# One staging ring of seven SBUF buffers, and the conversions' shifted word in PSUM throughout, in a fused attention, FFN and mixture-of-experts kernel

## The chip, the cores and the metric

The program runs on one core of one Trainium2 chip. The metric is the device time of one execution in microseconds (us). The kernel before takes 1338.55 us (median of 3 runs, 1336.74 to 1340.67). The engines are called PE (TensorE), DVE (VectorE), ACT (ScalarE), POOL (GpSimd) and SP (SyncE, which issues the DMAs here).

## What is computed

```python
scores = q @ k.T / sqrt(64)                       # 4 batches, 8 heads, 576 x 576
kth    = np.partition(scores, -32)[..., -32]      # the 32nd largest of each row
attn   = softmax(where(scores >= kth, scores, -1e9))
x      = (attn @ v) as 2304 rows of 512
x      = relu(x @ w_in) ** 2 @ w_out              # d_ff 2048, w_in and w_out in float64
# the two best of 8 experts of each row by noisy logits, and then
out   += weight * (relu(x @ w1[e]) @ w2[e])       # d_ff 1024
```

## The kernel before

**Attention.** The work is cut into 80 units; a unit is a pair of heads for one tile of 128 queries (or for the 64 left-over queries of a batch). Each head of a full unit, and each left-over unit as a whole, is one *search*, 144 in all: PE makes the scores (L439), ACT evacuates them (L442), DVE finds the 32nd largest (`max` L453, `match_replace` L457 and what follows, ending in a `reduce_max`, L494), POOL and ACT make the masked exponentials (POOL L506, ACT L510, POOL L511, ACT L512), PE transposes them (L523), ACT copies them out (L525), and PE multiplies by the values (L564).

**Staging of keys and queries.** Keys and queries are loaded in float32 into staging tiles, `kn` for two heads of keys (L408 and L409, two buffers) and `qn` for four heads of queries (L423 and L424, two buffers), and then split into a rounded high part (ACT, L400) and a remainder (DVE or POOL, L401). One `qn` serves the four searches of a tile's half of the heads; it is called a query group below.

**Conversions.** The FFN's weights come as float64. `convert` (from L144) makes float32 of one 128 by 512 block: a load of 512 KB into `raw` (four buffers), ACT scales the high words into a tile `high` (L153), DVE shifts `high` in place (L155) and joins the sign to it (L156), ACT scales the low words (L157), POOL adds them (L158), and SP stores the block to DRAM (`whole`, L159). There are 32 such conversions. For the first 14 (`IN_PSUM`), `high` is a bank of the pool `ps_acc` in PSUM (three banks in rotation); for the last 18 it is the SBUF tile `ca` itself.

**FFN.** It runs in seven chunks of 2, 2, 2, 3, 3, 3 and 3 tiles of 128 rows as background work between the steps of attention. Chunk 0 reads `whole` in float32 (L351, L315); chunk 1 reads `whole` into the same four `raw` buffers, splits it and stores the two parts (L336 to L342); later chunks read those. The accumulators of a chunk are banks of `ps_acc`, one for each tile, and so are the banks that `route` uses behind each chunk for its transposes and logits. Then come the experts (from 667 us).

**What sets the order.** Each engine runs its instructions in a fixed order, which is found when the program is built: the Python code gives instructions and priorities, a scheduler orders them by a timeline of its own, and buffers of a pool are given out in turn. All loads and stores of the lines above stand in one queue, SP's.

Of the kernel before, what the change touches and what calls it, by code (L numbers as in the profile page):

```python
# [8 lines left out]
F32 = mybir.dt.float32  # L9
# [18 lines left out]
CONVERTS = 3  # L28
IN_PSUM = 14
LEFT_WEIGHT = 0.6  # L30
# [24 lines left out]
def attention_ffn_moe(ctx: ExitStack, tc: tile.TileContext, q, k, v, w_ffn, w_route, noise, w_exp, out,  # L55
# [66 lines left out]
    ps_acc = wctx.enter_context(tc.tile_pool(name="ps_acc", bufs=3, space=PSUM))  # L122

    def late_consts():
        nc.sync.dma_start(wg, w_route)
        nc.sync.dma_start(nz, noise)
# [15 lines left out]


    def convert(vpool, f, which):  # L144
        n = DM
        raw = vpool.tile([P, 2 * n], U32, name="raw", bufs=4 if keep is not None else 2)
        nc.sync.dma_start(raw, w_ffn[f, which])
        pair = raw.rearrange("p (j t) -> p j t", t=2)
        lo_w, hi_w = pair[:, :, 0], pair[:, :, 1]
        a = vpool.tile([P, n], U32, name="ca", bufs=4 if keep is not None else 2)  # L150

        high = ps_acc.tile([P, DM], F32, name="acc") if 2 * f + which < IN_PSUM else a.bitcast(F32)
        nc.scalar.activation(high, hi_w.bitcast(F32), AF.Copy, scale=2.0 ** -112)  # L153
        high = high.bitcast(U32)
        nc.vector.tensor_scalar(high, high, 3, None, op0=ALU.logical_shift_left)  # L155
        nc.vector.scalar_tensor_tensor(a, hi_w, 0x80000000, high, op0=ALU.bitwise_and, op1=ALU.bitwise_or)  # L156
        nc.scalar.activation(lo_w, lo_w, AF.Copy, scale=2.0 ** -29)  # L157
        nc.gpsimd.tensor_tensor(a, a, lo_w, op=ALU.add)  # L158
        nc.sync.dma_start(whole[f][:, which], a.bitcast(F32))  # L159
# [27 lines left out]
    def route(t0, xrs):  # L187
# [3 lines left out]
        if after:  # L191
            bank = lambda: after[0].tile([P, DM], F32, name="acc2")
            xts = [mpools[0].tile([P, NC, P], F32, name="xts", bufs=CT) for _ in xrs]
        else:
            bank = lambda: ps_acc.tile([P, DM], F32, name="acc")
            xts = [fpool.tile([P, NC, P], F32, name="xt", bufs=2) for _ in xrs]
# [104 lines left out]
    def ffn(t0, nt, xT):  # L301
# [4 lines left out]
        def second(f, wo, gt):  # L306
            if f == 0:
                while fronts:
                    front()
                acc.extend(ps_acc.tile([P, DM], F32, name="acc") for _ in range(nt))  # L310
            for tt in range(nt):
# [14 lines left out]
        for f in range(NF):  # L326
# [7 lines left out]
            elif divide:  # L334
                raw = vpools[0].tile([P, 2 * DM], U32, name="raw", bufs=4 if keep is not None else 2).bitcast(F32)
                nc.sync.dma_start(raw, whole[f].rearrange("p a d -> p (a d)"))  # L336
# [66 lines left out]
    def prep_k(b, g, j):  # L403
# [3 lines left out]
        for h in ([2 * j], [2 * j + 1]) if (b, g) == (0, 0) else ([2 * j, 2 * j + 1],):  # L407
            kn = apool.tile([P, 2, S], F32, name="kn", bufs=2)[:, 0:len(h), :]  # L408
            nc.sync.dma_start(kn, k[b, 4 * g + h[0]:4 * g + h[-1] + 1].rearrange("h p s -> p h s"))  # L409
            dst = K4[b, g][:, h[0]:h[-1] + 1, :]  # L410
            for i in range(len(h)):
                split(nc.vector if (b, g) == (0, 0) else nc.gpsimd, dst[:, i], dst[:, i], kn[:, i], D)

# [7 lines left out]
    def prep_q(b, g, s0):  # L421

        qn = apool.tile([P, 4, P], F32, name="qn", bufs=2)  # L423
        nc.sync.dma_start(qn.rearrange("p h s -> p (h s)"), q[b, s0 // P, g])  # L424
# [227 lines left out]
    def expert(e, parts, ahead):  # L652
# [14 lines left out]
        for n, t in enumerate(tiles_):  # L667
            acc[t] = ps_acc.tile([P, DM], F32, name="acc") if n < 3 else ps_m.tile([P, DM], F32, name="acc2")

# [315 lines left out]
    def beyond(e, row):  # L985
# [23 lines left out]
        nc.scalar.copy(xt, pt.rearrange("p (c s) -> p c s", c=NC))  # L1009
        acc = ps_acc.tile([P, DM], F32, name="acc")  # L1010
        for f in range(NFE):
# [116 lines left out]
```

## Time and profile before

| | us |
|---|---|
| median of 3 runs | 1338.55 |
| the profiled execution, its own time | 1336.86 |
| its span in the trace | 1335.1 |
| PE busy | 1241.5 (93%) |
| DVE busy | 899.2 (67%) |
| ACT busy | 856.6 (64%) |
| POOL busy | 746.2 (56%) |
| mean granted PE clock | 0.985 of full speed |

The busy shares are averages over stages with different limits: in attention all engines are in use, in the experts' part mostly PE. The span lacks 1.8 us of the profiled execution's own time, which lie around it.

### The profile page before, as it was taken

How to read it: one execution, taken by the hardware profiler on the slowest of the kernel's cores; microseconds unless marked ns; L12 is line 12 of the kernel's file. 1: busy time of each engine (PE TensorE's matmuls, PEld its weight loads, DVE VectorE, ACT ScalarE, POOL GpSimd, SP SyncE). 2: the span in 40 equal slices, each digit the busy share in tenths (PEclk: the TensorE clock that was granted, in tenths of full speed). 3: DMA queues.
4: the chain of work that ended last, by engine and by line, in shares of the span. 5: the costliest groups of instructions: out<-in, count | busy, mean ns of one | idle time of the engine just before them, and what ended most of it. 6: DMA issues, size and time to landing. Idle time of an engine off the chain costs nothing.

```text
span 1335.1 us, 26136 instructions
## 1 busy us (share of the span) xinstructions
PE 1241.5 (93%) x8030; PEld 1071.8 (80%) x8030; DVE 899.2 (67%) x4557; ACT 856.6 (64%) x1886; POOL 746.2 (56%) x1243
## 2 busy tenths in 40 slices
PE   3769889989998999999999999999999999999997
PEld 2556667777887888888888888899899999988886
DVE  8999989998986899978677410255534343444554
ACT  6878879989897889987878653543433333332443
POOL 5857798887786676767655635333432241503221
PEclk9889999999999999999999999999999999999999
DMA  9998886875675554366534689366643443534464
GB/s 333 361 368 292 274 273 235 309 260 181 219 231 193 166 174 157 106 211 204 168 115 158 205 297 332 113 198 197 192 151 117 143 136 119 174 103 143 141 202 140
DMA packets 93302, 270.06 MB, mean 202 GB/s; under 512 B 11612, under 2 KB 11740, under 8 KB 93152
## 3 DMA queue, kind: packets, MB, share of 16 engines
q1 hardware_dynamic: 83872, 239.91, 54.3%
q0 software_dynamic: 9280, 28.40, 5.9%
q8 instruction: 65, 1.06, 0.3%
q14 instruction: 85, 0.70, 0.2%
HBM read 209.90 MB, written 60.45 MB: 202 GB/s over the span
## 4 chain that ended last, share of the span: by engine, by line
PE 61%; ACT 13%; DVE 11%; DMA 7%; issue 5%; POOL 3%; SPq 0%; POOLq 0%; DVEq 0%; ACTq 0%
PE pa L564 5%; PE ph L693 5%; PE ph L695 4%; PE ph L694 4%; PE acc L676 4%; PE acc L674 4%; PE acc L675 4%; PE ps L439 4%; PE pa L523 3%; PE acc L322 3%; PE acc L320 3%; PE acc L321 3%; DMA raww<-in_exp 3%; PE pf L357 2%; PE pf L358 2%
## 5 line engine op out<-in xcount | busy, mean ns | idle before, releaser
L511 POOL TENSOR_TENSOR sb<-sb,w 128x576 f32<-128x576 f32 x144 | 205.8, 1430 | 63.3 <-ACT w L510 59.3
L453 DVE MAX8 m<-sb 128x8 f32<-128x115 f32 (+1 forms) x720 | 190.3, 264 | 53.1 <-ACT sb L442 47.6
L457 DVE MATCH_REPLACE8 w<-m,sb 128x115 f32<-128x115 f32 (+1 forms) x720 | 187.1, 263 | 0.0
L699 ACT ACTIVATE ht<-ph 128x384 fp32r<-128x384 f32 (+1 forms) x128 | 55.8, 436 | 195.2 <-PE ph L695 177.0
L715 POOL DMA_INDIRECT out<-y,info x40 | 45.1, 1127 | 242.4 <-DVE y L714 224.7
L439 PE MATMUL ps<-K,qt 128*128 128x288 f32 (+2 forms) x640 | 131.4, 333 | 43.9 <-ACT sb L442 30.0
L700 DVE SCALAR_TENSOR_TENSOR ht<-ph,ht 128x384 fp32r<-128x384 f32 (+1 forms) x128 | 62.7, 490 | 161.7 <-ACT ht L699 148.5
L693 PE MATMUL ph<-xe,wi 128*128 128x256 f32 (+1 forms) x512 | 159.9, 312 | 1.9 <-ACT wi L686 1.0
L695 PE MATMUL ph<-xe,wi 128*128 128x256 f32 (+1 forms) x512 | 159.2, 311 | 0.2 <-DVE wi L687 0.2
L694 PE MATMUL ph<-xe,wi 128*128 128x256 f32 (+1 forms) x512 | 158.9, 310 | 0.0
L439 PEld LDWEIGHTS ps<-K,qt 128*128 128x128 f32 x640 | 103.7, 204 | 64.4 <-ACT sb L442 37.7
L512 ACT ACTIVATE sb<-sb,keep 128x576 f32<-128x576 f32 x144 | 112.5, 781 | 28.1 <-POOL sb L511 27.6
L674 PE MATMUL acc<-wo,ht 128*128 128x512 f32 x320 | 125.8, 397 | 0.4 <-DVE y L714 0.4
L675 PE MATMUL acc<-wo,ht 128*128 128x512 f32 x320 | 125.3, 395 | 0.0
L510 ACT ACTIVATE w<-sb,keep 128x576 f32<-128x576 f32 x144 | 111.3, 775 | 16.4 <-POOL keep L506 16.2
L371 POOL TENSOR_TENSOR gt<-r,gt 128x384 fp32r<-128x384 f32 (+1 forms) x96 | 90.7, 946 | 53.2 <-ACT gt L370 39.9
L481 DVE MAX8 m<-w 128x8 f32<-128x288 f32 x288 | 116.0, 443 | 0.1
L357 PE MATMUL pf<-xT,wi 128*128 128x384 f32 (+1 forms) x320 | 106.0, 331 | 5.4 <-ACT r L364 3.9
L523 PE MATMUL pa<-ident,sb 128*128 128x128 f32 x576 | 94.8, 289 | 16.5 <-ACT sb L512 7.1
L676 PE MATMUL acc<-wo,ht 128*128 128x512 f32 x320 | 108.9, 401 | 0.0
L525 ACT COPY pt<-pa 128x512 f32<-128x512 f32 x144 | 83.2, 578 | 32.1 <-PE pa L523 21.2
L693 PEld LDWEIGHTS ph<-xe,wi 128*128 128x128 f32 x512 | 96.4, 188 | 8.5 <-ACT wi L686 1.4
(211 smaller groups left out, 3511.9 us busy)
## 6 DMA issues: line engine op xcount, KB each, us to landing
raww<-in_exp SPq DMA_DIRECT2D x88, 512.0 KB
wi<-wsc SPq DMA_DIRECT2D x64, 512.0 KB
wo<-wsc SPq DMA_DIRECT2D x64, 512.0 KB
raw<-in_ffn SPq DMA_DIRECT2D x32, 512.0 KB
xs<-xr SPq DMA_DIRECT2D x40, 258.0 KB
mr<-xs SPq DMA_DIRECT2D x40, 258.0 KB
qn<-in_q SPq DMA_DIRECT2D x40, 256.0 KB
whole<-ca SPq DMA_DIRECT2D x32, 256.0 KB
```

What stands on the lines that cost most here:

```text
L357: nc.tensor.matmul(ph[:, 0:n], wi[:, 0, sl], xT[:, 0, c, 0:n], start=(c == 0), stop=False)
L439: nc.tensor.matmul(ps[:, n, 0:w], st, kt[:, at:at + w], start=(i == 0), stop=(i == len(pairs) - 1))
L453: in_turn(nc.vector.max(parts[i][1], sb[:, parts[i][0]]))
L457: in_turn(nc.vector.match_replace(out=w[:, sl], in_to_replace=top, in_values=sb[:, sl], imm_value=NEG))
L511: nc.gpsimd.tensor_tensor(sb, sb, w, op=ALU.subtract)
L523: nc.tensor.transpose(pt[:, c * P:(c + 1) * P], e[:, c * P:(c + 1) * P], ident)
L674: queued(nc.tensor.matmul(acc[t], hs[i][:, 0, sl], wo[:, 0, :], start=(f == 0), stop=False))
L675: queued(nc.tensor.matmul(acc[t], hs[i][:, 0, sl], wo[:, 1, :], start=False, stop=False))
L676: queued(nc.tensor.matmul(acc[t], hs[i][:, 1, sl], wo[:, 0, :], start=False, stop=(f == NFE - 1)))
L693: queued(nc.tensor.matmul(ph[:, 0:n], wi[:, 0, sl], xe[i][:, 0, c, :], start=(c == 0), stop=False))
L694: queued(nc.tensor.matmul(ph[:, 0:n], wi[:, 0, sl], xe[i][:, 1, c, :], start=False, stop=False))
L695: queued(nc.tensor.matmul(ph[:, 0:n], wi[:, 1, sl], xe[i][:, 0, c, :], start=False, stop=(c == NC - 1)))
```

## The change

All staging goes through one ring, `staged()`: seven buffers of 4 KB a partition under the name `raw`, used for the conversions' loads, for chunk 1's reading of `whole`, for keys (now one head to a buffer and to a DMA, where it was two) and for queries. The private buffers `kn` and `qn` are gone. The three banks of `ps_acc` are split into two that rotate (`acc`) and one by itself (`third`); `acc_bank(i)` gives the third for every third index. All 32 conversions now have `high` in PSUM: the first 12 (`ALL_BANKS`) in the three banks in turn, the other 20 in `third` alone, which chunks of two tiles don't use as accumulator.

```diff
--- before.py
+++ after.py
@@ -26,7 +26,7 @@
 K_AHEAD = [7, 6, 4, 3]
 V_AHEAD = 8
 CONVERTS = 3
-IN_PSUM = 14
+ALL_BANKS = 12
 LEFT_WEIGHT = 0.6
 FILLS = [0.02, 0.1, 0.15, 0.2, 0.15, 0.1, 0.2, 0.1]
 ROUTE_WAIT = 30
@@ -121,6 +121,11 @@
     ps_f = wctx.enter_context(tc.tile_pool(name="ps_f", bufs=1, space=PSUM))
     ps_acc = wctx.enter_context(tc.tile_pool(name="ps_acc", bufs=3, space=PSUM))
 
+    def acc_bank(i):
+        if i % 3 == 2:
+            return ps_acc.tile([P, DM], F32, name="third", bufs=1)
+        return ps_acc.tile([P, DM], F32, name="acc", bufs=2)
+
     def late_consts():
         nc.sync.dma_start(wg, w_route)
         nc.sync.dma_start(nz, noise)
@@ -141,15 +146,19 @@
                 yield
 
 
+    def staged():
+        return vpools[0].tile([P, 2 * DM], U32, name="raw", bufs=7 if keep is not None else 4)
+
     def convert(vpool, f, which):
         n = DM
-        raw = vpool.tile([P, 2 * n], U32, name="raw", bufs=4 if keep is not None else 2)
+        raw = staged()
         nc.sync.dma_start(raw, w_ffn[f, which])
         pair = raw.rearrange("p (j t) -> p j t", t=2)
         lo_w, hi_w = pair[:, :, 0], pair[:, :, 1]
         a = vpool.tile([P, n], U32, name="ca", bufs=4 if keep is not None else 2)
 
-        high = ps_acc.tile([P, DM], F32, name="acc") if 2 * f + which < IN_PSUM else a.bitcast(F32)
+        n_conv = 2 * f + which
+        high = acc_bank(n_conv if n_conv < ALL_BANKS else 2)
         nc.scalar.activation(high, hi_w.bitcast(F32), AF.Copy, scale=2.0 ** -112)
         high = high.bitcast(U32)
         nc.vector.tensor_scalar(high, high, 3, None, op0=ALU.logical_shift_left)
@@ -192,7 +201,8 @@
             bank = lambda: after[0].tile([P, DM], F32, name="acc2")
             xts = [mpools[0].tile([P, NC, P], F32, name="xts", bufs=CT) for _ in xrs]
         else:
-            bank = lambda: ps_acc.tile([P, DM], F32, name="acc")
+            turn = iter(range(10))
+            bank = lambda: acc_bank(next(turn))
             xts = [fpool.tile([P, NC, P], F32, name="xt", bufs=2) for _ in xrs]
         for xr, xt in zip(xrs, xts):
             turned(bank, xr, xt, last)
@@ -307,7 +317,7 @@
             if f == 0:
                 while fronts:
                     front()
-                acc.extend(ps_acc.tile([P, DM], F32, name="acc") for _ in range(nt))
+                acc.extend(acc_bank(i) for i in range(nt))
             for tt in range(nt):
                 sl = slice(tt * P, (tt + 1) * P)
                 if plain:
@@ -332,7 +342,7 @@
                 for i, w in enumerate((wi, wo)):
                     nc.sync.dma_start(w[:, 0, :].bitcast(F32), whole[f][:, i])
             elif divide:
-                raw = vpools[0].tile([P, 2 * DM], U32, name="raw", bufs=4 if keep is not None else 2).bitcast(F32)
+                raw = staged().bitcast(F32)
                 nc.sync.dma_start(raw, whole[f].rearrange("p a d -> p (a d)"))
                 for i, (w, eng) in enumerate(((wi, nc.gpsimd), (wo, nc.vector))):
                     part = raw[:, i * DM:(i + 1) * DM]
@@ -405,11 +415,11 @@
         if j == 0:
             K4[b, g] = apool.tile([P, 4, S], F32R, name="K4", bufs=3)
         for h in ([2 * j], [2 * j + 1]) if (b, g) == (0, 0) else ([2 * j, 2 * j + 1],):
-            kn = apool.tile([P, 2, S], F32, name="kn", bufs=2)[:, 0:len(h), :]
-            nc.sync.dma_start(kn, k[b, 4 * g + h[0]:4 * g + h[-1] + 1].rearrange("h p s -> p h s"))
             dst = K4[b, g][:, h[0]:h[-1] + 1, :]
             for i in range(len(h)):
-                split(nc.vector if (b, g) == (0, 0) else nc.gpsimd, dst[:, i], dst[:, i], kn[:, i], D)
+                kn = staged().bitcast(F32)[:, 0:S]
+                nc.sync.dma_start(kn, k[b, 4 * g + h[i]])
+                split(nc.vector if (b, g) == (0, 0) else nc.gpsimd, dst[:, i], dst[:, i], kn, D)
 
     def prep_v(b):
         V[b] = []
@@ -420,7 +430,7 @@
 
     def prep_q(b, g, s0):
 
-        qn = apool.tile([P, 4, P], F32, name="qn", bufs=2)
+        qn = staged().bitcast(F32)[:, 0:4 * P].rearrange("p (h s) -> p h s", h=4)
         nc.sync.dma_start(qn.rearrange("p h s -> p (h s)"), q[b, s0 // P, g])
         qt = apool.tile([P, 2, 4, P], F32R, name="qt", bufs=3)
         split(nc.vector if b == 0 and s0 == 0 else nc.gpsimd, qt[:, 0], qt[:, 1], qn, 0)
@@ -665,7 +675,7 @@
                 bounds_check=NT - 1, oob_is_err=False)
         acc = {}
         for n, t in enumerate(tiles_):
-            acc[t] = ps_acc.tile([P, DM], F32, name="acc") if n < 3 else ps_m.tile([P, DM], F32, name="acc2")
+            acc[t] = acc_bank(n) if n < 3 else ps_m.tile([P, DM], F32, name="acc2")
 
         def second(f, wo, hs):
             for t in tiles_:
@@ -1007,7 +1017,7 @@
             nc.tensor.transpose(pt[:, c * P:(c + 1) * P], xr[:, c * P:(c + 1) * P], ident)
         xt = opool.tile([P, NC, P], F32, name="xto")
         nc.scalar.copy(xt, pt.rearrange("p (c s) -> p c s", c=NC))
-        acc = ps_acc.tile([P, DM], F32, name="acc")
+        acc = acc_bank(0)
         for f in range(NFE):
             raw = mpool.tile([P, 2, DM], F32, name="raww", bufs=3)
             nc.sync.dma_start(raw, w_exp[e, f])
```

How instructions move is seen in each engine's order of instructions. The first place is SP's queue where the third tile's first query group is loaded (`qn_796` before, `raw_800` now; `xs` and `out` stores fill buffers in DRAM with zeros). Before:

```order
L409 DMA kn_259<-in_k 128x2x576
L136 DMA xs<-xr_1641 128x516
L409 DMA kn_265<-in_k 128x2x576
L418 DMA vt_1816<-in_v 128x512
L424 DMA qn_525<-in_q 128x512
L424 DMA qn_796<-in_q 128x512
L136 DMA xs<-xr_1641 128x516 x2
```

Now:

```order
L144 DMA out<-xr_1661 128x512 x4
L168 DMA whole2<-ca_511 128x512
L155 DMA raw_790<-in_ffn 128x1024
L343 DMA wo_1481<-whole0 128x512
L144 DMA out<-xr_1661 128x512
L434 DMA raw_800<-in_q 128x512
L168 DMA whole2<-ca_521 128x512
```

The load was the 28th DMA of the queue and is the 92nd; by the shapes of the rows, 8.5 MB were issued ahead of it and 26.9 MB are now. The 12 conversion loads up to `raw_790` stand ahead of it, where it were four.

The second place is ACT's order where that query group is split. Before it stood behind the 8th evacuation of scores (L442):

```order
L510 ACTIVATE w_231<-sb_191,keep_58 128x576
L442 ACTIVATE sb_401<-ps_442 128x576
L400 ACTIVATE qt_798<-qn_796 128x512
L553 COPY t5_480<-pa_477 128x256
L153 ACTIVATE acc_508<-raw_505 128x512
```

Now it stands between the 16th evacuation and the 17th (L452), which needs it, and among the steps of the 15th search's softmax (`w_955`, `sb_948`):

```order
L520 ACTIVATE w_955<-sb_948,keep_58 128x576
L563 COPY t5_1298<-pa_1295 128x256
L410 ACTIVATE qt_802<-raw_800 128x512
L522 ACTIVATE sb_948,sm_947<-sb_948,keep_58 128x576
L535 COPY pt_1354<-pa_1349 128x512
L452 ACTIVATE sb_1086<-ps_1087 128x576
L452 ACTIVATE sb_1086<-ps_1127 128x576
```

The third place is DVE's order from the end of the 15th search (the `TENSOR_REDUCE`) to its first step on the 17th (`m_1094`), now:

```order
L504 TENSOR_REDUCE m_956<-m_956 128x1
L467 MATCH_REPLACE w_995<-m_996,sb_948 128x115 x2
L164 TENSOR_SCALAR third_793<-third_793 128x512
L165 SCALAR_TENSOR_TENSOR ca_772<-raw_770,acc_773 128x512
L541 TENSOR_TENSOR xT_497<-pa_1300,t5_1298 128x128
L463 MAX m_1094<-sb_1086 128x8
```

So few instructions lie between the two there. Counted over DVE's whole order, the last conversion's join stands behind the 28th search, where it stood behind the 32nd; in PE's order chunk 0's first layer has 36 matmuls behind it after the 12th unit, where it had 32, and 60 after the 15th, where it had 56. From the 17th unit on PE's order is nearly the same row for row.

## Rows read from the trace of the kernel before

**Rows 1.** The profile page, part 1: busy time, share, instructions of each engine.
```profile
PE 1241.5 (93%) x8030; PEld 1071.8 (80%) x8030; DVE 899.2 (67%) x4557; ACT 856.6 (64%) x1886; POOL 746.2 (56%) x1243
```

**Rows 2.** Windows by stage: length, busy us of each engine, granted clock, DMA share, GB/s.
```profile
0.00:97.70 97.70, 52.93 (x312) 41.58 (x312) 92.26 (x542) 75.29 (x149) 63.84 (x95) 0.89 1.02 357
97.70:204.80 107.10, 96.61 (x527) 67.99 (x528) 99.41 (x492) 88.83 (x203) 85.48 (x89) 0.94 0.83 277
204.80:300.00 95.20, 85.37 (x679) 71.98 (x678) 91.15 (x549) 87.21 (x211) 82.16 (x125) 1.00 0.77 270
300.00:667.00 367.00, 351.00 (x2656) 306.24 (x2656) 310.32 (x2103) 314.67 (x733) 269.10 (x427) 1.00 0.55 182
667.00:1335.10 668.10, 655.54 (x3860) 583.97 (x3858) 306.02 (x873) 290.63 (x593) 245.59 (x511) 1.00 0.52 169
```

**Rows 3.** Timeline of PE, end of chunk 0: start, us, instruction, count.
```profile
194.06 1.89 PE L351 MATMUL pf<-xT,wi 128*128 128x256 f32 x8
195.79 1.88 PE L315 MATMUL acc<-wo,gt 128*128 128x512 f32 x4
...
204.84 0.68 PE L357 MATMUL pf<-xT,wi 128*128 128x256 f32 x1
```

**Rows 4.** The chain that ended last, 0 to 340 us: start, us, what.
```profile
152.33 1.82 DVE ca L156
```

**Rows 5.** Groups by form, DVE, 0 to 200 us: count, busy us, mean ns, idle.
```profile
L156 DVE SCALAR_TENSOR_TENSOR ca<-raw,ca 128x512 uint32<-128x512 uint32 x18 | 18.1, 1007 | 0.0
L155 DVE TENSOR_SCALAR ca<-ca 128x512 uint32<-128x512 uint32 x18 | 14.7, 818 | 0.0
...
L155 DVE TENSOR_SCALAR acc<-acc 128x512 uint32<-128x512 uint32 x14 | 9.5, 681 | 0.0
L156 DVE SCALAR_TENSOR_TENSOR ca<-raw,acc 128x512 uint32<-128x512 uint32 x14 | 9.4, 670 | 0.0
```

**Rows 6.** Lines L155 and L156: ns of one (min/median/max), first and last start.
```profile
L155 DVE TENSOR_SCALAR ca<-ca x18: 400/590/1564, 112.4 to 180.5; 128x512 uint32<-128x512 uint32 x18
...
L156 DVE SCALAR_TENSOR_TENSOR ca<-raw,ca x18: 664/676/1896, 113.1 to 182.8; 128x512 uint32<-128x512 uint32 x18
```

**Rows 7.** Windows of 20 us, columns as in rows 2.
```profile
0.00:20.00 20.00, 5.28 (x16) 3.92 (x16) 14.82 (x59) 13.03 (x21) 7.88 (x32) 1.00 0.92 317
20.00:40.00 20.00, 10.31 (x44) 8.18 (x46) 19.74 (x125) 14.43 (x29) 17.09 (x19) 1.00 1.06 359
40.00:60.00 20.00, 14.67 (x98) 11.28 (x94) 20.00 (x118) 17.56 (x38) 15.14 (x17) 0.83 1.05 364
60.00:80.00 20.00, 13.74 (x80) 11.45 (x81) 20.00 (x141) 15.77 (x34) 14.91 (x19) 0.66 1.02 353
```

**Rows 8.** Timeline of SP: when the query loads went out.
```profile
20.75 1.75 SPq L424 DMA_DIRECT2D qn<-in_q  x2
```

**Rows 9.** Windows of L494 alone (one for each finished search).
```profile
0.00:82.00 82.00, 2.09 (x15) 0.88 1.01 350
```

**Rows 10.** Groups of the page, part 5, and POOL by form, 0 to 100 us (L506).
```profile
L511 POOL TENSOR_TENSOR sb<-sb,w 128x576 f32<-128x576 f32 x144 | 205.8, 1430 | 63.3 <-ACT w L510 59.3
...
L523 PE MATMUL pa<-ident,sb 128*128 128x128 f32 x576 | 94.8, 289 | 16.5 <-ACT sb L512 7.1
...
L512 ACT ACTIVATE sb<-sb,keep 128x576 f32<-128x576 f32 x144 | 112.5, 781 | 28.1 <-POOL sb L511 27.6
...
L510 ACT ACTIVATE w<-sb,keep 128x576 f32<-128x576 f32 x144 | 111.3, 775 | 16.4 <-POOL keep L506 16.2
...
L525 ACT COPY pt<-pa 128x512 f32<-128x512 f32 x144 | 83.2, 578 | 32.1 <-PE pa L523 21.2
...
L506 POOL TENSOR_TENSOR keep<-m,cb 128x4 f32<-128x4 f32 x19 | 3.7, 197 | 4.2 <-DVE m L494 4.0
```

**Rows 11.** Timeline of ACT at the start: a split of keys, an evacuation of scores.
```profile
5.95 0.68 ACT L400 ACTIVATE K<-kn 128x576 fp32r<-128x576 f32 x1 [1.01 <-DMA kn<-in_k]
7.15 0.65 ACT L442 ACTIVATE sb<-ps 128x576 f32<-128x576 f32 x1 [0.52 <-PE ps L439]
```

## The prediction

> **What bounds the kernel now.** I read the page first: PE is busy 93% of the span [rows 1], so at most 7% can go, unless PE is given less work, which the change doesn't do. Then the windows by stage, to see where that idle time lies [rows 2]. Until 97.7 us PE is idle for 44.8 us, because chunk 0's input isn't there before eight units of attention are done. From 97.7 to 204.8 us chunk 0 runs between the units: PE idles 10.5 us and DVE 7.7 us. From 204.8 to 300 us PE idles 9.8 us and DVE 4.0 us; later PE is busy 95.6% and 98% of the time. The reader should see that the first two stages hold most of what can still move. Once chunk 1 has begun, the same work follows in nearly the same order, so a later or earlier beginning of chunk 1 shifts the rest.
>
> What paces those two stages is DVE: in each 20 us from 20 to 80 us it is busy 19.74 us and more [rows 7]. But two others are near their end. The DMA share is 1.0 up to 97.7 us [rows 2, 7], and from 97.7 us on PE is busy 90% of the time. The close of the second stage is PE's: the timeline shows chunk 0's blocks one behind the other up to 204.84 us, where chunk 1's first matmul starts [rows 3]. Last I looked at the conversions, which lie on the chain that ended last with stretched instructions, such as a join of 1.82 us [rows 4].
>
> **The change part by part.** The sum is made against the profiled execution's 1336.86 us (span 1335.1 and 1.8 around it), which is 1.7 below the median of the runs shown, 1338.55.
>
> *The shifted word.* With `high` in PSUM a shift takes 681 ns and a join 670; with `high` in SBUF they take 818 and 1007 on the mean [rows 5], though the quickest take 400 and 664 and the slowest 1564 and 1896 [rows 6]. POOL was busy 80% of that stage [rows 2] with instructions on SBUF, and the PSUM form shows no such spread, so I read the excess as waiting for POOL's accesses. All 18 conversions that change take the PSUM form: 18 x (1007 - 670) = 6.1 us and 18 x (818 - 681) = 2.5 us, together 8.5 us less on DVE, in a stage where DVE is the pacer.
>
> The rule that speaks against it: the Trainium skill (VectorE: DVE Perf Modes, "Why PSUM operands drop a tier") says that an operand in PSUM caps a float32 operation at the slowest rate, since the fast mode of a one-input operation needs both read ports of SBUF. The quickest shift, 400 ns against 681, agrees; by that rule alone the shifts would cost 18 x 281 ns = 5.1 us more instead of 2.5 less, and the sum below would end near 1336.
>
> *One bank for 20 conversions.* Each holds `third` for ACT's write, the shift and the join, some 0.7 + 0.68 + 0.67 = 2.1 us. DVE's order has these 20 within 12 searches; 15 searches with 8 conversions among them were done by 82 us [rows 9], 5.5 us each, so the 20 have over 60 us, 3 us each. I take nothing: the searches' steps between cover the wait for ACT. Without that cover the 20 would take 42 us in a row.
>
> *The start.* Four heads of keys are now split by ACT ahead of the first evacuation, where it were two: 2 x 0.68 us [rows 11]. Since DVE must do its part of those splits anyhow, the loss lies between 0 and 1.4; I take 1.
>
> *Queries through the ring.* The third tile's first query group was loaded at about 21 us [rows 8] and now has 26.9 MB ahead of it in SP's queue. In the first 80 us, 20 x (317 + 359 + 364 + 353) GB/s = 27.9 MB moved [rows 7], so it lands near 78 us. Before, the 15th search was done by 82 us [rows 9]; with the start's 1 us and two to four more conversions ahead of it (1.35 us each) that is 86 to 88 us now. So the group is there in time, but the 17th search still stalls: its evacuation stands in ACT's order behind the softmax of the 15th. From that search's end the chain is L506 0.20, L510 0.78, L511 1.43, L512 0.78, four transposes 4 x 0.165 (94.8 us over 576), L525 0.58 [rows 10] and the evacuation 0.65 [rows 11]: 5.1 us. DVE has a shift, a join and three small steps for that time (third order excerpt), some 2.1 us. Loss 3 us; the ends are 0, if later DVE work had been late anyhow, and 16, if two groups land late (below).
>
> *Chunk 0 further ahead.* PE's order has one block of chunk 0 more behind the 12th to 15th units, because conversions now end four searches earlier. A block is 1.89 + 1.88 = 3.8 us [rows 3], and it goes from the close of the stage, where DVE waits, into the time before. Gain 3.8 us; the ends are 0 and the 7.7 us that DVE idles there [rows 2].
>
> *Keys of one head each* add 14 DMA issues on SP, off any path. Batch 1's keys are loaded and split later, but still ahead of the 37th search. Seven buffers for chunk 1's weights may take part of DVE's 4.0 us idle of the third stage [rows 2]; I count nothing. The banks of route and the accumulators stay three in number; with `third` fixed, an accumulator of the next chunk can wait for one copy more, under 1 us (L525's size [rows 10]) at three chunks, hidden by attention's matmuls.
>
> *Sum.* -8.5 + 1 + 3 - 3.8 = -8.3 us. But PE ends the second stage, and its work there stays 96.6 us. Its idle time can't vanish: at the 4.4% that it keeps from 300 to 667 us [rows 2], 4.7 of its 10.5 us stay, so at most 5.8 go. I take 5.8: 1336.86 - 5.8 = **1331 us**. About 0.3% (4 us) is what a measurement of this kernel can tell from no change.
>
> **The rivals.**
> - *The others pace it, no change: 1337.* ACT is busy 88.8, POOL 85.5 and PE 96.6 of the second stage's 107.1 us [rows 2]. If PE's waits for ACT and POOL stay as they are, DVE's freed 8.5 us show as idle time in front of its searches. For it: the close of the stage is PE's. Against: DVE's idle time is 7% of the stage, less than that of any other. Chance 0.26.
> - *The ring starves the searches, slower: 1344.* Conversions take the ring's buffers, and each query group waits for a buffer and stands behind their loads. If the 26.9 MB move at the second stage's 277 GB/s instead of 350, the group lands at 98 us; needed at 87, it costs 11 us, and the next group, behind it in the ring, some 5 more: -8.3 + 16 = +7.7. It decides from the point at which the group lands after the 15th search ends, about 86 us. For it: eight more conversion loads stand ahead. Against: at a DMA share of 1.0 the stores and loads ahead of it flow at 350 GB/s [rows 7]. Chance 0.12.
> - *The waits move, the shift's own time stays, slower: 1342.* If an instruction that no longer waits inside only waits in front of the next one, since POOL has the same work to do, then what remains is 400 against 681 ns: 1336.9 + 5.1. By the skill's rule above that is the shift's whole effect. Against: the join in PSUM form never took over 680 ns beside a busy POOL. Chance 0.06.
> - *PE doesn't cap it, faster still: 1321.* If the conversions that were late are what PE waited for, DVE's 8.5 us and its 7.7 us of idle time both go: 1336.9 - 16.2. Chance 0.06.
>
> **How the numbers follow.** The forecast has a chance of 0.50. Faster is it and the last rival, 0.56; the same 0.26; slower 0.12 + 0.06 = 0.18. Of the forecast's own range, the gain is between 2 (a stall of 5 and no block ahead) and 10.5 (all of PE's idle time): 1326 to 1335. To hold 8 in 10 the range takes in most of both sides: low 1320, the large gain; high 1343, the slower cases but for their worst.
>
> **What would show it.** The 18 shifts and joins at about 680 and 670 ns. DVE's busy time up to chunk 1's beginning some 8 us shorter. The last conversion's join at about 160 us instead of 183. A gap of about 3 us in DVE near 87 us, waiting for an evacuation. Chunk 1's first matmul near 199 us instead of 204.84, and the rest of the span unchanged. The forecast is wrong if that matmul comes after 203 us, if DVE's idle time in the second stage grows instead, or if a wait for a query load shows in the chain.

## The result, and the profile after

The change takes **1349.54 us** (median of 5 runs, 1347.56 to 1352.37) against 1338.55 for the kernel before in the same comparison: ratio 1.0083, 95% interval 1.0061 to 1.0104. It is slower by 0.8%, where 1331 us, with a range up to 1343, was forecast. The profiled execution took 1349.54 us with a span of 1347.7.

The first part of the page after, the busy times, beside [rows 1]:

```profile
PE 1246.1 (92%) x8030; PEld 1076.0 (80%) x8030; DVE 887.6 (66%) x4557; ACT 859.9 (64%) x1886; POOL 746.3 (55%) x1243
```

DVE works 11.6 us less than before, as intended, and the span is 12.6 us longer. The windows by stage say where: up to 97.7 us as in [rows 2] (chunk 0's own first matmul comes at 102.1, before at 102.2), to chunk 1's first matmul (207.0, before 204.8), to chunk 2's (319.7), chunk 3's (417.8) and chunk 4's (558.7).

```profile
core 0: us, PE busy (x) PEld busy (x) DVE busy (x) ACT busy (x) POOL busy (x), PEclk, DMA share, GB/s
0.00:97.70 97.70, 56.27 (x299) 42.76 (x299) 87.46 (x496) 72.52 (x140) 56.26 (x87) 0.79 1.01 352
97.70:207.00 109.30, 97.95 (x545) 69.72 (x544) 95.95 (x537) 92.26 (x208) 84.56 (x97) 0.94 0.81 277
207.00:319.70 112.70, 96.13 (x760) 80.64 (x759) 102.35 (x625) 99.28 (x239) 95.19 (x135) 0.98 0.72 251
319.70:417.80 98.10, 90.82 (x755) 79.38 (x754) 84.05 (x578) 85.95 (x213) 78.74 (x128) 1.00 0.64 209
417.80:558.70 140.90, 130.75 (x963) 114.22 (x962) 116.61 (x796) 117.46 (x267) 99.07 (x157) 0.99 0.52 173
```

The same stages of the kernel before, between the first matmuls of its chunks:

```profile
204.80:310.60 105.80, 95.38 (x760) 79.88 (x759) 101.75 (x613) 97.53 (x237) 90.40 (x136) 1.00 0.76 267
310.60:409.70 99.10, 93.06 (x757) 80.71 (x755) 85.08 (x577) 86.09 (x212) 81.10 (x131) 0.98 0.64 211
409.70:546.90 137.20, 129.12 (x964) 112.78 (x962) 117.95 (x808) 117.22 (x267) 96.09 (x154) 1.00 0.50 165
```

Chunk 1's stage, 112.7 us, is 6.9 longer for the same PE work (96.1 against 95.4): PE idles 16.6 us in it, before 10.4. Chunk 3's is 3.7 longer. The stage ahead of chunk 1 ends 2.2 later, not 6 earlier. Behind 558.7 us little more is lost: 789.0 us to the end against 788.2.

The conversions themselves do what was forecast. DVE's groups by form, in the first 207 us:

```profile
L164 DVE TENSOR_SCALAR third<-third 128x512 uint32<-128x512 uint32 x24 | 16.5, 687 | 0.2
L165 DVE SCALAR_TENSOR_TENSOR ca<-raw,third 128x512 uint32<-128x512 uint32 x24 | 16.2, 673 | 0.0
```

A shift takes 687 ns and a join 673, against 818 and 1007 with the word in SBUF [rows 5].

**First loss, the searches.** The third tile's first query group (the `raw` load from `in_q`) is issued at 73.21 us; before it was the second of the two loads of [rows 8], which were issued from 20.75 us on. This is SP's timeline:

```profile
73.21 0.38 SPq L434 DMA_DIRECT2D raw<-in_q  x1
```

and these are DVE's rows at the 17th search:

```profile
82.98 0.70 DVE L165 SCALAR_TENSOR_TENSOR ca<-raw,acc 128x512 uint32<-128x512 uint32 x1
86.58 0.29 DVE L541 TENSOR_TENSOR xT<-pa,t 128x128 f32<-128x128 f32 x1 [2.90 <-PE pa L574]
89.15 0.28 DVE L463 MAX8 m<-sb 128x8 f32<-128x116 f32 x1 [2.28 <-ACT sb L452]
```

DVE stands still for 2.90 and 2.28 us. What it waits for is in ACT's rows: the split of the query group (L410) waits for nothing, the softmax of the 15th search (L522) and its transposes, which ACT copies out (L535), come next, and the 17th search's evacuation (L452) last:

```profile
83.91 0.63 ACT L410 ACTIVATE qt<-raw 128x512 fp32r<-128x512 f32 x1
85.27 0.78 ACT L522 ACTIVATE sb<-sb,keep 128x576 f32<-128x576 f32 x1 [0.73 <-POOL sb L521]
87.98 0.59 ACT L535 COPY pt<-pa 128x512 f32<-128x512 f32 x1 [1.84 <-PE pa L533]
88.46 0.66 ACT L452 ACTIVATE sb<-ps 128x576 f32<-128x576 f32 x1
```

The windows of 20 us from 40 to 140 us, beside [rows 7] up to 80, show PE in that time:

```profile
40.00:60.00 20.00, 14.11 (x90) 11.10 (x90) 20.00 (x117) 15.83 (x33) 11.93 (x15) 0.66 1.05 361
60.00:80.00 20.00, 11.11 (x74) 7.94 (x70) 20.00 (x135) 13.30 (x28) 8.87 (x13) 0.68 1.04 365
80.00:100.00 20.00, 11.15 (x54) 8.26 (x56) 14.82 (x79) 14.41 (x29) 11.53 (x13) 0.59 0.94 339
100.00:120.00 20.00, 15.12 (x74) 11.17 (x72) 20.00 (x97) 18.00 (x38) 14.47 (x15) 0.84 0.90 315
120.00:140.00 20.00, 19.44 (x104) 14.08 (x105) 19.97 (x105) 17.77 (x40) 15.38 (x17) 0.87 0.91 297
```

and the kernel before, in the third of them:

```profile
80.00:100.00 20.00, 11.21 (x95) 8.76 (x94) 20.00 (x119) 16.80 (x37) 10.67 (x14) 0.92 1.00 379
```

DVE is busy 14.82 of 20 us in the third window. PE runs 54 matmuls there, before 95; its granted clock is 0.59, so mostly the lower of its two levels, and 0.84 to 0.87 in the 40 us behind it. The clock was low before the stall, too (0.68 in the window ahead of it, in the kernel before 0.66); what differs is that it rises later.

**Second loss, chunk 1's stage.** POOL's timeline, where chunk 0's rows are scattered:

```profile
295.81 0.97 POOL L282 DMA_INDIRECT xs<-xr,si  x1 [0.30 <-issue]
300.67 1.39 POOL L411 TENSOR_TENSOR K<-raw,K 64x576 fp32r<-64x576 f32 x1 [3.89 <-DMA xs<-xr,si]
302.14 0.72 POOL L381 TENSOR_TENSOR gt<-r,gt 128x256 fp32r<-128x256 f32 x1
```

and the waits of all engines from 288 to 306 us (total, times, longest):

```profile
DVE wo L351 <- ACT wo L350: 7.0, 1, 7.0
PE acc L332 <- POOL gt L381: 5.5, 1, 5.5
ACT w L520 <- POOL keep L516: 5.4, 1, 5.4
POOL K L411 <- DMA xs<-xr,si: 3.9, 1, 3.9
```

A split of batch 2's keys stands behind the four scatters and waits until they have landed. Behind it on POOL stands the `gt` for which PE waits, and all four engines stop. Before, the first four heads of batch 2 were split together, 95 us ahead of chunk 0's scatters:

```profile
193.92 5.52 POOL L401 TENSOR_TENSOR K<-kn,K 64x576 fp32r<-64x576 f32 x4
```

In the ring, among chunk 1's weights, they come at 284.85 us (the first) and from 300.67 on.

**Third loss, chunk 3's beginning.** PE waits at 420.6 us for the last `wo` of chunk 2 (waits from 406 to 428 us):

```profile
PE acc L330 <- DMA wo<-wsc: 4.4, 1, 4.4
```

### The profile page after: what moved, and what is told of

It is laid out like the page before. It is cut to its first block, busy times and chain, and to the rows that moved or that the text cites. A ratio compares the mean times of both kernels' runs of the same rounds, so it can differ in the third digit from the quotient of the medians.

```text
span 1347.7 us, 26133 instructions
## 1 busy us (share of the span) xinstructions
PE 1246.1 (92%) x8030; PEld 1076.0 (80%) x8030; DVE 887.6 (66%) x4557; ACT 859.9 (64%) x1886; POOL 746.3 (55%) x1243
## 4 chain that ended last, share of the span: by engine, by line
PE 61%; ACT 8%; DVE 7%; DMA 7%; POOL 4%; issue 3%; SPq 0%; POOLq 0%; DVEq 0%; ACTq 0%; another core or an unknown queue 0%
PE ph L703 5%; PE ph L705 5%; PE ph L704 5%; PE pa L574 4%; PE acc L684 4%; PE acc L685 4%; PE acc L686 4%; PE ps L449 4%; PE pa L533 3%; DMA raww<-in_exp 3%; PE pf L367 2%; PE pf L368 2%; PE pf L369 2%; PE acc L332 2%; PE acc L330 2%
## 5 line engine op out<-in xcount | busy, mean ns | idle before, releaser
L521 POOL TENSOR_TENSOR sb<-sb,w 128x576 f32<-128x576 f32 x144 | 206.5, 1436 | 67.4 <-ACT w L520 63.3
L522 ACT ACTIVATE sb<-sb,keep 128x576 f32<-128x576 f32 x144 | 112.2, 779 | 26.1 <-POOL sb L521 25.6
L533 PE MATMUL pa<-ident,sb 128*128 128x128 f32 x576 | 96.8, 293 | 14.1 <-ACT sb L522 12.6
L367 PE MATMUL pf<-xT,wi 128*128 128x384 f32 (+1 forms) x320 | 104.9, 328 | 0.8 <-ACT r L374 0.8
L703 PEld LDWEIGHTS ph<-xe,wi 128*128 128x128 f32 x512 | 96.3, 188 | 7.4 <-ACT wi L696 1.9
L368 PE MATMUL pf<-xT,wi 128*128 128x384 f32 (+1 forms) x320 | 101.6, 318 | 0.2 <-issue 0.2
L684 PE MATMUL acc<-wo,ht 128*128 128x512 f32 x256 | 100.3, 396 | 1.6 <-DVE y L724 1.6
L369 PE MATMUL pf<-xT,wi 128*128 128x384 f32 (+1 forms) x320 | 101.6, 317 | 0.0
L704 PEld LDWEIGHTS ph<-xe,wi 128*128 128x128 f32 x512 | 96.3, 188 | 4.9
```

The lines of the kernel that those rows point to most:

```text
L367: nc.tensor.matmul(ph[:, 0:n], wi[:, 0, sl], xT[:, 0, c, 0:n], start=(c == 0), stop=False)
L368: nc.tensor.matmul(ph[:, 0:n], wi[:, 0, sl], xT[:, 1, c, 0:n], start=False, stop=False)
L369: nc.tensor.matmul(ph[:, 0:n], wi[:, 1, sl], xT[:, 0, c, 0:n], start=False, stop=(c == NC - 1))
L521: nc.gpsimd.tensor_tensor(sb, sb, w, op=ALU.subtract)
L533: nc.tensor.transpose(pt[:, c * P:(c + 1) * P], e[:, c * P:(c + 1) * P], ident)
L684: queued(nc.tensor.matmul(acc[t], hs[i][:, 0, sl], wo[:, 0, :], start=(f == 0), stop=False))
```

## The experiments

All were run beside the kernel before; ratios are to it, and the kernel before moves by up to 4 us from one comparison to another, so that times of different comparisons are compared by ratio. Beginnings and lengths of stages in us are read from the profiled execution (a chunk begins with its first `pf` matmul); "rest" is from chunk 4's beginning to the end of the span. A profiled execution lies up to 4 us from the median of its kernel (e6's 3.7 above it, e4's 3.2 below).

| run | chunk 0 | chunk 1 | its stage | chunk 2's | chunk 3's | rest | ratio (95%) |
|---|---|---|---|---|---|---|---|
| before | 102.2 | 204.8 | 105.8 | 99.1 | 137.2 | 788.2 | 1 |
| the change | 102.1 | 207.0 | 112.7 | 98.1 | 140.9 | 789.0 | 1.0083 (1.0061-1.0104) |
| e1 banks alone | 102.1 | 201.9 | 107.6 | 104.5 | 135.1 | 789.1 | 1.0033 (1.0021-1.0044) |
| e2 ring alone | 103.6 | 214.4 | 113.6 | 100.8 | 140.2 | 787.3 | 1.0160 (1.0138-1.0183) |
| e3 own q | 97.6 | 198.5 | 115.4 | 97.2 | 138.4 | 788.2 | 1.0019 (1.0008-1.0030) |
| e4 keys early | 102.5 | 206.5 | 117.3 | 103.8 | 135.7 | 787.9 | 1.0153 (1.0132-1.0173) |
| e5 own k | 118.5 | 217.4 | 110.1 | 101.9 | 135.3 | 789.7 | 1.0150 (1.0134-1.0166) |
| e6 own both | 116.6 | 211.2 | 105.2 | 96.4 | 139.2 | 796.7 | 1.0082 (1.0066-1.0098) |
| e7 own q, old banks | 97.2 | 204.6 | 115.8 | 98.6 | 136.2 | 786.0 | 1.0076 (1.0063-1.0089) |
| e8 mixed | 98.0 | 197.8 | 106.9 | 95.8 | 138.6 | 792.5 | 0.9987 (0.9979-0.9996) |
| e9 own q, 36 for all | 97.9 | 197.8 | 106.5 | 97.1 | 142.9 | 792.8 | 1.0049 (1.0036-1.0062) |
| e10 change, 36 for all | 103.1 | 209.4 | 107.4 | 97.5 | 141.2 | 792.0 | 1.0096 (1.0080-1.0112) |
| e11 own q, 36 for chunk 0 | 98.5 | 199.9 | 106.8 | 100.3 | 136.3 | 788.6 | 0.9970 (0.9956-0.9984) |
| e12 change, 36 for chunk 0 | 101.9 | 207.4 | 107.4 | 99.9 | 142.8 | 789.1 | 1.0092 (1.0075-1.0110) |

**e1 and e2, each half alone.** e1 gives keys and queries their buffers back and the ring four; e2 gives the banks their old rotation (the change's lines on banks undone).

```diff
-        return vpools[0].tile([P, 2 * DM], U32, name="raw", bufs=7 if keep is not None else 4)
+        return vpools[0].tile([P, 2 * DM], U32, name="raw", bufs=4 if keep is not None else 2)
...
-        qn = staged().bitcast(F32)[:, 0:4 * P].rearrange("p (h s) -> p h s", h=4)
+        qn = apool.tile([P, 4, P], F32, name="qn", bufs=2)
...
+            kn = apool.tile([P, 2, S], F32, name="kn", bufs=2)[:, 0:len(h), :]
```

> The banks and the shifted word in PSUM stay as in the change; keys and queries have their own buffers again (kn, qn, two each) and the ring has four buffers. Theory A (the loss of 11 us lies in the ring: keys' splits that get behind the scatters, the stall before the 17th search, loads that come together): 1337 us, between 1333 and 1340, batch 2's key splits ahead of chunk 0's scatters, no gap of 4 us on PE after 250 us, chunk 1 beginning near 205 us, since DVE's 8.5 us show as idle time. Rival B (the banks cost it: one bank for all late conversions, third fixed in route and in the accumulators): 1345 to 1350, chunk 1 beginning at 207 us or later. Rival C (the shorter shifts and joins are worth their 8.5 us, and only the ring hid it): 1330.

> The ring of seven for conversions, keys and queries as in the change; the banks in their old rotation of three and the shifted word in PSUM for the first 14 conversions alone. Theory A (the ring): 1349 us, between 1345 and 1354, with the wait of a key split for the scatters of chunk 0 near 295 us and a PE gap of about 5 us behind it, and a stall of 3 to 6 us before the 17th search. Rival B (the banks): 1338 to 1341, and the gap near 300 us either absent or without effect on the start of chunk 2. Rival C (PSUM form worth 8.5 us): 1357.

Measured: e1 1340.67 us, ratio 1.0033; e2 1358.13, ratio 1.0160. The ring is the half that costs, more than the whole change: with it, the PSUM form is worth 7.4 us up to chunk 1's beginning (214.4 against 207.0), so rival B falls and C is nearest in e2. Theory A's range is missed in both, in e1 by 0.7 us. In e1 the banks alone gain 2.9 us by chunk 1's beginning but are 4.3 us behind by chunk 3's (414.0 against 409.7); that loss has no single wait and stays open.

**e3, queries out of the ring.**

```diff
-        qn = staged().bitcast(F32)[:, 0:4 * P].rearrange("p (h s) -> p h s", h=4)
+        qn = apool.tile([P, 4, P], F32, name="qn", bufs=2)
...
-        return vpools[0].tile([P, 2 * DM], U32, name="raw", bufs=7 if keep is not None else 4)
+        return vpools[0].tile([P, 2 * DM], U32, name="raw", bufs=6 if keep is not None else 4)
```

> As the change, but queries have their own two buffers (qn) again and the ring has six. Theory A with the keys as its costlier part: the stall before the 17th search goes (5.2 us of DVE waits), chunk 1 begins 1 to 2 us earlier than 207, the wait of the key split for the scatters and the gap of 5.5 us stay: 1347, between 1344 and 1350. Rival D (it is the queries that cost it): 1338 to 1341. Rival B (the banks): 1349.

Measured: 1339.24, ratio 1.0019: D, not A. Chunk 0 begins 4.5 us earlier than in the change and chunk 1 8.5 earlier, at the 199 us that had been forecast. Its windows from 60 to 120 us, the stall gone and the clock up:

```profile
60.00:80.00 20.00, 12.10 (x77) 9.50 (x76) 20.00 (x141) 13.93 (x30) 11.37 (x15) 0.76 1.04 375
80.00:100.00 20.00, 15.35 (x113) 12.53 (x112) 19.39 (x117) 15.68 (x33) 12.45 (x15) 0.83 0.86 314
100.00:120.00 20.00, 16.68 (x87) 11.23 (x86) 20.00 (x108) 18.65 (x43) 15.29 (x18) 1.00 0.87 294
```

But chunk 1's stage is longer still, 115.4 us, with the same wait of a key split for the scatters (3.8 us) and a PE gap of 6.3 us behind it. e3 differs from the change in one buffer of the ring, too. Whether a ring with more buffers would do as well with the queries in it wasn't run.

**e4, keys taken up earlier.**

```diff
-K_AHEAD = [7, 6, 4, 3]
+K_AHEAD = [10, 9, 7, 6]
```

> As the change, with one constant changed: K_AHEAD is 10, 9, 7, 6 where it is 7, 6, 4, 3, so that a batch's keys take their places in the ring three units earlier. Batch 2's first four key splits then stand ahead of chunk 0's scatters in POOL's order, and none right behind them. Theory A: the PE gap of 5.5 us near 300 us goes, and chunk 2 begins near 313 to 315 us instead of 319.7: 1344 us, between 1341 and 1347. If the scatter wait is only where time shows that is lost anyway (rival E: PE had to wait for attention's later searches in any case), the gap moves to another wait and the time stays 1349. Rival B (the banks): 1349.

Measured: 1356.08, a miss for all three. The wait for the scatters is gone, but chunk 1's stage takes 117.3 us, and PE waits for DVE's part of chunk 1's weights instead (waits from 300 to 324 us):

```profile
PE acc L331 <- DVE wo L351: 4.9, 1, 4.9
```

That the keys, now earlier in the ring, hold up the loads of these weights is the likely reason; it isn't shown.

**e5, keys out of the ring** (as e1's line for `kn`, ring of five), **and e6, both out** (queries as in e3; keys in two buffers of one head; ring of five).

> As the change, but keys have their own buffers (kn, two of two heads, one load for both) again and the ring has five; queries stay in it. Theory F (two losses, one for each user of the ring: queries in the ring cost 8 us before chunk 1 begins, 207.0 against 198.5 without; keys in it cost 6 to 9 us in chunk 1's stage, through the split behind the scatters): chunk 1 begins at 205 to 209 us, its stage takes 105 to 108 us and no key split waits for the scatters of chunk 0: 1343, between 1340 and 1346. Rival D (the queries alone cost it; what is lost in chunk 1's stage would be lost without keys in the ring too): 1349.

> As the change, but queries have their own two buffers, keys two of one head each, and the ring of conversions' loads has five. Theory F: both losses go, the gain forecast for the shifted word shows: chunk 1 begins at 198.5 to 201 us, its stage takes 105 to 108 us, no PE gap over 4 us: 1332, between 1329 and 1336, so faster than the kernel before (1337). Rival G (what chunk 1's stage gives or takes evens out what the stage ahead gained, since attention's searches, not chunk 1's weights, pace it up to 310 us): chunk 1 begins early but chunk 2 at 310 us as before: 1337 to 1340, as with the banks alone (1340.7).

Measured: 1356.13 and 1346.74, both misses in the total, and both of use by stage. In e5 the smaller ring makes the queries' wait worse: the query group that the change issues at 73.21 us comes at 87.14, the 16th search ends at 104 us instead of 93, and chunk 0 begins at 118.5. That is the rival "the ring starves the searches", reached with five buffers. SP's timeline of e5, and ACT's wait of 4.34 us for that load:

```profile
87.14 0.44 SPq L434 DMA_DIRECT2D raw<-in_q  x1
```

```profile
94.65 0.63 ACT L410 ACTIVATE qt<-raw 128x512 fp32r<-128x512 f32 x1 [4.34 <-DMA raw<-in_q]
```

In e6 the start pays: with two small buffers, the loads of batch 0's last two heads of keys stand far behind in SP's order, and are issued 11 us and more after the splits of the two heads before them ended (at 27.6 and 29.3 us); the 8th search ends at 63.9 us, in e3 at 51.5, and chunk 0 begins at 116.6:

```profile
40.48 0.33 SPq L421 DMA_DIRECT2D kn<-in_k  x1
42.59 0.33 SPq L421 DMA_DIRECT2D kn<-in_k  x1
```

Yet in e6 chunk 1's stage takes 105.2 us: without keys in the ring that loss is gone.

**e7, the PSUM form without queries in the way** (e3 with e2's banks).

> Queries in their own two buffers, keys in the ring of six, the banks in their old rotation and the shifted word in PSUM for the first 14 conversions alone: the run with its own query buffers (1339.2, chunk 1 from 198.5 us) without the PSUM half of the change. Theory H (the PSUM form is worth what it was worth between the change and the ring alone, 207.0 against 214.4): chunk 1 begins near 206 us and the time is 1346 to 1349. Rival A (PE, ACT and POOL pace the stage, and the PSUM form shows as idle time on DVE once queries come in time): chunk 1 begins at 198 to 201 us, 1338 to 1342.

Measured: 1345.10, ratio 1.0076, chunk 1 at 204.6: nearest to theory H, 0.9 us under its range. Against e3 the PSUM form is worth 6.1 us up to there. The key split waits 6.4 us for the scatters here and PE's gap is 10.8 us, yet chunk 1's stage, 115.8 us, is about as long as e3's (115.4): the length of the gap is not the length lost.

**e8, both out, but batch 0's keys through the ring** (e6, with this line).

```diff
-                kn = staged().bitcast(F32)[:, 0:S]
+                kn = staged().bitcast(F32)[:, 0:S] if b == 0 else apool.tile([P, S], F32, name="kn", bufs=2)
```

> As the change, but queries have their own two buffers; batch 0's keys go through the ring, which has five, and the keys of later batches have two buffers of one head each. So the first tile's keys no longer wait for buffers (in the run with two one-head buffers for all keys chunk 0 began 14 us late) and no key split waits for chunk 0's scatters. Theory F: chunk 0 begins at 97 to 99 us, chunk 1 at 198 to 202, its stage takes 105 to 108: 1331, between 1327 and 1336. Rival G (searches pace chunk 1's stage, so that an early beginning is lost by 310 us): 1337 to 1340.

Measured: 1332.83, ratio 0.9987, within theory F's range: chunk 1 at 197.8, its stage 106.9. Of the 7.8 us ahead at chunk 4's beginning 4.3 are lost in the rest (792.5 us); from 712 to 852 us no wait of PE is over 1.5 us, so that no single cause can be named.

**e9 and e10, the scatters later** (e3 and the change).

```diff
-ROUTE_WAIT = 30
+ROUTE_WAIT = 36
```

> As the run with own buffers for queries and a ring of six (1339.2, chunk 1 from 198.5 us, its stage 115.4), with one constant changed: ROUTE_WAIT is 36 where it is 30, so that the scatters of chunk 0 stand behind all four key splits of batch 2 in POOL's order. Nothing else of the ring changes. Theory F: the wait of 3.8 us and PE's gap of 6.3 us behind it go, the stage takes 107 to 110 us, 1333, between 1330 and 1336. Rival G or E (PE finds the time lost at another wait): 1338 to 1341.

> As the change itself, with ROUTE_WAIT 36 where it is 30: chunk 0's scatters behind the key splits of batch 2 in POOL's order. Theory F: PE's gap of 5.5 us at 297 us goes, chunk 1 still begins at 207 us, chunk 2 at 314 us: 1344, between 1341 and 1347. Rival E (as with the keys taken up earlier, which removed the wait and took its time elsewhere): 1349 to 1356.

Measured: 1340.99 and 1348.53, the first within rivals G and E, the second between theory F and rival E. Chunk 1's stage shrinks as theory F says, from 115.4 to 106.5 us and from 112.7 to 107.4; the total doesn't. But the constant moves every chunk's route, and the rest grows to 792.8 and 792.0; in e10 chunk 1 also begins 2.4 us later.

**e11 and e12, the scatters of chunk 0 alone later** (e3 and the change).

```diff
-        yield LAST_WAIT if after else ROUTE_WAIT
+        yield LAST_WAIT if after else 36 if t0 == 0 else ROUTE_WAIT
```

> As the run with own query buffers (1339.2), but only chunk 0's route yields 36 before its second part; all other chunks keep 30. Theory L (with 36 for every chunk the stage of chunk 1 gained its 9 us, 106.5 against 115.4, and the later chunks' moved routes gave them back: 142.9 against 138.4 in chunk 3's stage, 4 us more in chunks 4 to 6): now the gain stays, 1332, between 1329 and 1335. Rival K (what is gained by chunk 2's beginning is given back later whatever moves it, because PE finds attention's products or the weights not ready in chunks 3 to 6): chunk 2 begins near 304 us, and the time is 1338 to 1341.

> As the change itself, with 36 for chunk 0's route alone. Theory L: chunk 1's stage 107 us instead of 112.7, the rest as in the change: 1344, between 1341 and 1347. Rival K: 1347 to 1350, with the 3 to 5 us lost again after chunk 3's beginning.

Measured: e11 1333.58, ratio 0.9970, theory L, and the lowest ratio of all (e8's 0.9987 is not clearly apart from it); against e3 the wait behind the scatters cost 0.49%, some 6.5 us. POOL's timeline of e11, the last key split and the first scatter:

```profile
292.10 1.42 POOL L411 TENSOR_TENSOR K<-raw,K 64x576 fp32r<-64x576 f32 x1
...
305.09 1.22 POOL L282 DMA_INDIRECT xs<-xr,si  x1 [0.20 <-DVE m L504]
```

e12 1348.42, ratio 1.0092: rival K. Chunk 1's stage gains 5.3 us, and chunk 2's and 3's lose 3.7 of them. e12 and e11 differ in where queries are staged (and in one buffer of the ring), and by 1.2%. 7.5 us of that lie before chunk 1 (207.4 against 199.9) and 6.5 in chunk 3's stage. SP's timeline and PE's longest wait in e12 show the third loss:

```profile
412.06 2.79 SPq L428 DMA_DIRECT2D vt<-in_v  x5
414.95 0.39 SPq L355 DMA_DIRECT2D wo<-wsc  x1
```

```profile
PE acc L330 <- DMA wo<-wsc: 4.9, 1, 4.9
```

and in e11 the order is the other way round (its last `wo` of chunk 2 is the load at 403.44 us), with no such wait:

```profile
403.44 0.32 SPq L355 DMA_DIRECT2D wo<-wsc  x1
...
405.86 1.85 SPq L428 DMA_DIRECT2D vt<-in_v  x4
```

Five loads of values (1.3 MB) stand ahead of chunk 2's last `wo` load in SP's queue in the one case, behind it in the other. In e2 and e4 it is ahead of them, too, and PE has no such gap; in e10 it is, and PE waits 4.7 us for the values instead. But the wait isn't all of chunk 3's stage: e2 and e9 take 140.2 and 142.9 us for it without such a gap.

## Why the prediction was wrong

The forecast was some 18.5 us short (1349.54 against 1331). 8.0 us of that lie ahead of chunk 1's first matmul (207.0 against 199); the rest lies behind it, where the forecast had no loss and the change takes 10.4 us longer than the kernel before.

- **Queries through the ring, "Loss 3 us", is the step that failed first.** Place and kind were right: the group landed in time (ACT splits it at 83.91 us, without waiting for its load), and the 17th search stalls because its evacuation stands behind the 15th's softmax. The stall is 5.2 us, because the chain from the 15th search's end to the evacuation's took 7.1 us (82.0 to 89.1) and not 5.1: the softmax's first step on ACT began at 82.98, behind a copy, and the transposes were ready 1.8 us after the softmax instead of 0.66, behind other matmuls at a granted clock of 0.54 (84 to 88 us). And the price doesn't end there: e3 shows 8.5 us by chunk 1's beginning, 4.5 ahead of chunk 0 and 4.0 in the stage behind it, where PE had been busy 90% already and the late units' matmuls come on top (524 matmuls from 102.1 to 207.0 us, in e3 511 from 97.6 to 198.5) at a granted clock of 0.95 against 0.98. Within the bounds of 0 to 16, but the value taken was the stall alone, and too small. In the sum it had no effect at all: without it the terms add to -11.3, and the cap makes the same 5.8 of that. In the runs it comes on top: e3 begins chunk 1 6.3 us ahead of the kernel before, the change 2.2 behind.
- **Keys, "off any path", failed too.** "Loaded and split later, but still ahead of the 37th search" was said of batch 1's. Batch 2's weren't looked at: their splits moved behind chunk 0's scatters on POOL and waited for them. e3 against e11: 6.5 us. With the queries in the ring, taking the wait away gains nothing in the total (e10 1.0096 and e12 1.0092, the change 1.0083). The seven buffers, of which "I count nothing" was said for chunk 1's weights, were shared with these keys.
- **"The rest of the span unchanged" failed.** A changed place in the ring alters the scheduler's order far behind. So the third loss, a wait of 4.4 us at chunk 3's beginning, came at a place the prediction never looked at. With queries out of the ring it is gone (e12 against e11); with them in it it is there in the change and in e12, but e2, e4 and e5 show no such gap. It is an order that the ring can lead to, not one that it must. The losses behind chunk 1's beginning don't add up, either: from there to the end the change takes 10.4 us more than the kernel before, e3 (queries out) and e12 (scatters later) 8.9 each, e11 (both) 1.7. Why one of the two alone saves so little there stays open; e1, without either user in the ring, loses 5.9.
- **The shifted word, -8.5 us, capped at 5.8, came out near its size, but not by the way forecast.** e3 against e7 gives 6.1 us and the change against e2 7.4, as soon as conversions' loads have six or seven buffers. With four (e1) 2.9 remain. On DVE it went as forecast: up to chunk 1's beginning it is busy 183.4 us, before 191.7, and the last join comes at 163.0 us. But the 5.8 were to come out of PE's idle time in the second stage, which was to fall from 10.5 us to 4.7, and it didn't. The stage from chunk 0's first matmul to chunk 1's, before, in the change, in e3 and in e7:

```profile
102.20:204.80 102.60, 92.14 (x501) 64.12 (x500) 94.91 (x469) 84.89 (x194) 82.54 (x86) 0.96 0.85 281
102.10:207.00 104.90, 94.87 (x524) 67.53 (x523) 91.55 (x517) 88.15 (x200) 81.69 (x93) 0.95 0.81 277
97.60:198.50 100.90, 90.35 (x511) 64.40 (x509) 91.89 (x501) 86.75 (x198) 81.62 (x93) 0.98 0.88 295
97.20:204.60 107.40, 94.46 (x505) 66.34 (x504) 97.90 (x503) 87.83 (x198) 87.50 (x93) 0.93 0.81 275
```

PE idles 10.5 us before, 10.0 in the change and 10.6 in e3. From e7 to e3 the stage is 6.5 us shorter: 2.4 of PE's idle time and 4.1 of its busy time, at a granted clock of 0.98 instead of 0.93. And 4.6 of the 6.3 us that e3 gains on the kernel before lie ahead of chunk 0, where e7, without the PSUM form, gains 5.0. So that e3 begins chunk 1 at 198.5 us, where 199 was forecast, is in part luck. The rival with the waits moved falls: the joins stay at 673 ns beside POOL. By the rule of the Trainium skill (VectorE: DVE Perf Modes, "Why PSUM operands drop a tier") alone the shifts would have cost 5.1 us more. The rule's tier is seen in the quickest shift in SBUF, 400 ns [rows 6], but the mean beside a busy POOL decides here, and the time agrees with the mean.

- **The rivals.** "The others pace it" holds for the second stage by itself, where PE's idle time stays. "The ring starves the searches" had the right side and the right user of the ring, by a mechanism, a group that lands late, which only e5's five buffers show. (In its working, 26.9 MB at 277 GB/s take 97 us, not 98.)
- **The smaller steps.** One bank for 20 conversions cost ACT 2.2 us of waits from 84 to 120 us, off any path that could be seen. The start cost 1.3 us, where 1 was taken: the first evacuation comes at 8.43 us, before at 7.15. The 15th search ended at 82.0 us, not at 86 to 88; before it was 79.8. The block of chunk 0 further ahead, 3.8 us, doesn't show in the change: by 97.7 us PE has run 299 matmuls, before 312; in e3 and e7 it is 337. When the last join ran, 27 searches had ended, not 28.

## What to carry to other kernels

A shared ring ties each user's place in its order to all the others': before merging private buffers, list for every user what stands ahead of it in the ring, and look at each place where its consumer is moved behind something slow in an in-order queue, over the whole program and not only near the change. Buffers for loads that a pacing engine needs on time (queries here) are worth keeping private; e11 takes the PSUM form and a ring of six without the queries, with batch 2's first four key splits kept ahead of the scatters, and beats the kernel before by 0.3% and the change by 1.1%. And an edit's value is best read stage by stage: several runs here gained 5 to 9 us in one stage and showed nothing in the total.

## What was not expected

The first key split behind chunk 0's scatters waits for the scatters' DMAs, though it reads nothing of theirs; in e4 a split of `wi` stands right behind them and starts at once. It costs 3.9 us on POOL, and the last scatter took 4.6 us from its issue to its landing in the chain of waits. The wait is in the program: in the traces of the change, e2, e3 and e7 the split has waits for the four scatters' semaphores in front of it. Why it has them isn't known from these runs. And a stall of 5 us on DVE at 83 to 89 us goes with a granted PE clock of 0.59, which is not back at 1.00 by 140 us (0.87), where e3 has 1.00 from 100 us on. That the stall is what holds the clock down isn't shown: from 80 to 83.6 us, ahead of it, the clock was 0.50 already.
